# Dealing out a gated block matmul by matmul in an attention kernel, with a new order of the work on GpSimd

## The chip, the cores and the metric

The kernel runs on one core of a Trainium2 chip. The metric is the device time in microseconds (us) of one execution, as the median of several runs. A run is called slow when it is over 1.5% above the fastest run of the same kernel. Engines are called PE (TensorE; PEld is its weight load), DVE (VectorE), ACT (ScalarE), POOL (GpSimd) and SP (SyncE, which issues DMAs). The granted clock is the share of its full clock that PE was given.

## The reference

Eight batches of attention with twelve heads (448 rows, 64 columns), q and k normalized by their root mean square; the heads, put side by side, feed a gated two-layer block whose gate mixes the rows.

```python
q_n, k_n = rmsnorm(q, g_q), rmsnorm(k, g_k)
attn = softmax(q_n @ k_n.T / 8)                 # per head
x = heads_side_by_side(attn @ v)                # (8, 448, 768)
h = relu(x @ w_in)                              # w_in 768 x 1024
u, v = h[..., :512], h[..., 512:]
v_n = (v - mean(v)) / sqrt(var(v) + 1e-6)       # over the 512 columns
v_s = w_spatial @ v_n + b_spatial[:, None]      # mixes the 448 rows
out = (u * v_s) @ w_out                         # w_out 512 x 768
```

## The kernel before

Heads are handled in 24 groups `G` of four, and each group in four steps `n`; one step is a round of the loop over `t`, with `G, n = divmod(t, 4)`. Twelve steps are a batch. Step `t` does the scores and the exponential of one head; around it, the loop queues, in program order on every engine, the preparation of later groups, the sums and values of the group before, and the gated block of the batch before.

A group's q and k go through five stages: `squares` (POOL), `reduce` (DVE), `rstd` (ACT), `scaled` (POOL), then a transpose by DMA; k has a last scaling by column, `k_scale` (DVE). The pieces that the argument touches:

```python
def load_v(b):                                   # 672 KB, issued by POOL
    pool.dma_start(out=t..., in_=v[b]...)

def squares(G, i, ..., eng=None):                # i = 0: q, 1: k
    (eng or pool).tensor_tensor(out=t, in0=x, in1=x, op=ALU.mult)
def reduce(G, i, ...):
    dve.tensor_reduce(out=sqs[G, l0][:, i, :], in_=sqt.pop((G, i, l0))..., op=ALU.add)
def scaled(G, i, ..., eng=None):
    (eng or pool).tensor_tensor(out=t..., in0=raw[G, i, l0]..., in1=rst[G, l0]..., op=ALU.mult)
def transpose_dma(G, i):
    sync.dma_start_transpose(out=t..., in_=nrm[G, i, 0]...)
def k_scale(G):                                  # bf16, from and to SBUF
    dve.tensor_scalar(out=kT, in0=krs.pop(G), scalar1=g2_col, ..., op0=ALU.mult)

def ln_apply(b):                                 # vn: bf16, from and to SBUF, four times
    for c in range(NC):
        dve.tensor_scalar(out=vn_t[b % 2][0:P, c, :], in0=vs[b][:, c, :],
                          scalar1=sts[b][:, c, 0:1], scalar2=rvs[b][:, c:c + 1],
                          op0=ALU.subtract, op1=ALU.mult)
```

The order inside the loop, steady stage:

```python
if n == 3 and G > 2 and G % NG == 0 and G // NG + 1 < B:      # NG = 3 groups a batch
    load_v(G // NG + 1)
A, R, T, K = G + 3, G + 2, G + 2, G + 1
if n == 2 and 5 <= K < NGT:  k_scale(K)
if n == 2 and 6 <= A < NGT:  squares(A, 0)
if n == 3 and 6 <= A < NGT:  squares(A, 1); reduce(A, 0)
if n == 0 and 6 <= R < NGT:  reduce(R, 1)
if n == 1 and 6 <= T < NGT:  rstd(T); scaled(T, 0); scaled(T, 1); transpose_dma(T, 0); transpose_dma(T, 1)
# then: sums at n == 0, values at n == 1 and 2, and the gated block in twelve unequal parts, one a step
```

The softmax here doesn't subtract the row's maximum and nothing guards it: scores larger than these inputs give would overflow.

## Time and profile before

| | before |
|---|---|
| time, median of 4 runs | 337.65 us (336.75 to 339.86) |
| span of the profiled run (fast), mean granted clock | 335.8 us, 0.937 |
| one batch in the steady stage, from exponential to exponential | 35.16 us |
| PE busy in such a batch | 33.64 us |

The prediction below shows the lines and how to read them. One more view, the group of `vn` in the list of groups (busy us, mean ns of one, idle before):

```profile
L331 DVE TENSOR_SCALAR vn<-vs,mv,rv 112x512 bf16<-112x512 bf16 x32 | 13.6, 483 | 0.7 <-ACT rv L326 0.6
```

### The profile page before, as it was taken

The numbers are of one execution on the slowest core, as the hardware profiler recorded it, in microseconds if no ns is written. First come the engines' busy times: TensorE is split into PE (matmuls) and PEld (weight loads), VectorE is DVE, ScalarE is ACT, GpSimd is POOL, SyncE is SP. The second block draws the span as 40 slices with busy tenths as digits, with TensorE's granted clock in tenths as the row PEclk, the third lists the DMA queues.
The fourth block names the chain that finished last, engine by engine and source line by source line (L and its number), as shares of the span: only waits on it lengthen the run. The fifth ranks groups of instructions, "written<-read, shape, count | busy, mean of one in ns | idle before, by whom it ended". The sixth has DMA issues, their size and how long they took to land.

```text
span 335.8 us, 6167 instructions
## 1 busy us (share of the span) xinstructions
PE 298.2 (89%) x2484; PEld 144.9 (43%) x2484; DVE 222.2 (66%) x364; ACT 223.5 (67%) x275; POOL 187.5 (56%) x114
## 2 busy tenths in 40 slices
PE   6757674789999989998999899989998999999993
PEld 6432231434444435443454344434543354435552
DVE  3667754566964977497757877588658964735551
ACT  4648495047877687778687768777877877784331
POOL 5824699747468648665956774795487454000000
PEclk9678595659999999999999999999999999999999
DMA  7993969928458994799389966895679254002205
GB/s 187 241 238 73 187 148 208 207 37 154 111 133 206 190 212 86 206 203 238 68 209 191 183 155 193 174 208 145 171 191 197 49 129 119 27 2 82 84 0 167
DMA packets 75061, 50.45 MB, mean 150 GB/s; under 512 B 36911, under 2 KB 71440, under 8 KB 75032
## 3 DMA queue, kind: packets, MB, share of 16 engines
q1 hardware_dynamic: 61792, 41.76, 53.9%
q0 software_dynamic: 13232, 8.30, 17.9%
q8 instruction: 19, 0.31, 0.4%
q14 instruction: 10, 0.08, 0.1%
q10 hardware_dynamic: 8, 0.00, 0.0%
HBM read 38.58 MB, written 11.01 MB: 148 GB/s over the span
## 4 chain that ended last, share of the span: by engine, by line
POOL 33%; issue 28%; PE 22%; DVE 6%; DMA 6%; ACT 3%; ACTq 0%; POOLq 0%; DVEq 0%; SPq 0%
POOL sqt L167 19%; POOL n L189 11%; PE ps L311 4%; DMA bst<-in_moe_b_spatial_dram 4%; PE ps L364 3%; PE ps L340 3%; PE ps L285 2%; PE pss L234 2%; PE ps L266 2%; ACT et L244 2%; PE ps L350 2%; POOL vt L80 2%; DVE n L189 1%; PE pse L234 1%; PE ps L200 1%
## 5 line engine op out<-in xcount | busy, mean ns | idle before, releaser
L244 ACT ACTIVATE et<-pss 112x1792 bf16<-112x1792 f32 x84 | 139.6, 1662 | 58.4 <-PE pss L234 57.5
L189 POOL TENSOR_TENSOR n<-qf,rs 112x1024 bf16<-112x1024 f32 x22 | 45.9, 2086 | 88.2 <-ACT rs L181 76.4
L173 DVE TENSOR_REDUCE ms<-sqt 112x16 f32<-112x1024 f32 x46 | 55.6, 1215 | 45.2 <-POOL sqt L167 45.2
L364 PE MATMUL ps<-w_out,gt 128*112 128x384 bf16 x256 | 47.6, 330 | 2.9 <-DVE osb L369 2.6
L234 PE MATMUL pss<-qT,kT 64*112 64x448 bf16 x304 | 44.5, 369 | 5.8 <-ACT et L244 5.2
L311 PE MATMUL ps<-w_in_v,xt 128*112 128x512 bf16 x192 | 49.3, 404 | 0.0
L285 PE MATMUL ps<-et,vt 112*32 112x448 bf16 x768 | 46.1, 361 | 0.0
L167 POOL TENSOR_TENSOR sqt<-qf 112x1024 f32<-112x1024 f32 x22 | 42.6, 1934 | 0.0
L167 POOL TENSOR_TENSOR sqt<-kf 112x1024 f32<-112x1024 f32 x22 | 41.7, 1895 | 1.3 <-DMA kf<-in_k_dram 1.2
L340 PE MATMUL ps<-xt,w_in_u 128*128 128x448 bf16 x192 | 40.1, 354 | 0.0
L364 PEld LDWEIGHTS <-gt 128*112 128x112 bf16 x256 | 31.2, 129 | 19.9 <-issue 12.5
L293 DVE TENSOR_TENSOR xt<-ps,rc 128x448 bf16<-128x448 f32 x48 | 29.3, 615 | 15.5 <-PE ps L285 15.5
L189 POOL TENSOR_TENSOR n<-kf,rs 112x1024 bf16<-112x1024 f32 x19 | 38.8, 2040 | 0.0
L311 PEld LDWEIGHTS <-xt 128*112 128x112 bf16 x192 | 24.6, 137 | 21.1 <-issue 9.5
L369 DVE COPY osb<-ps 112x384 f32<-112x384 f32 x46 | 24.4, 552 | 7.6 <-PE ps L364 5.1
L234 PEld LDWEIGHTS <-kT 64*112 64x112 bf16 x304 | 14.9, 124 | 31.7 <-issue 31.4
L285 PEld LDWEIGHTS <-vt 112*32 112x32 bf16 x768 | 16.3, 97 | 25.4 <-issue 17.1
L350 PE MATMUL ps<-w_spT,vn 112*128 112x448 bf16 (+1 forms) x128 | 26.9, 353 | 0.0
L244 ACT ACTIVATE et<-pse 112x896 bf16<-112x896 f32 x24 | 20.5, 913 | 9.6 <-PE pse L234 9.5
L340 PEld LDWEIGHTS <-w_in_u 128*128 128x128 bf16 x192 | 17.1, 98 | 20.9 <-issue 7.2
L266 PE MATMUL ps<-et,ones 112*32 112x448 bf16 x384 | 24.8, 382 | 0.0
L317 DVE BATCH_NORM_STATS2 s<-vs 112x6 f32<-112x512 bf16 x32 | 21.7, 680 | 2.5 <-ACT vs L301 2.5
(59 smaller groups left out, 276.0 us busy)
## 6 DMA issues: line engine op xcount, KB each, us to landing
out_dram<-osb SPq DMA_DIRECT2D x31, 336.0 KB, 3.0
qf<-in_q_dram SPq DMA_DIRECT2D x23, 448.0 KB, 8.1
kf<-in_k_dram SPq DMA_DIRECT2D x23, 448.0 KB, 7.3
vt<-in_v_dram POOLq DMA_DIRECT2D x8, 672.0 KB, 13.1
w_in_v<-in_moe_w_in_dram POOLq DMA_DIRECT2D x4, 192.0 KB, 5.8
w_in_u<-in_moe_w_in_dram POOLq DMA_DIRECT2D x4, 192.0 KB, 8.0
w_out<-in_moe_w_out_dram POOLq DMA_DIRECT2D x1, 768.0 KB, 13.4
f<-in_q_dram SPq DMA_DIRECT2D x2, 224.0 KB, 4.0
```

Source lines behind the costliest of these rows:

```text
L167: (eng or pool).tensor_tensor(out=t, in0=x, in1=x, op=ALU.mult)
L173: dve.tensor_reduce(out=sqs[G, l0][:, i, :], in_=sqt.pop((G, i, l0)).rearrange("p l (c d) -> p (l c) d", d=D), axis=AX.X, op=ALU.add)
L189: (eng or pool).tensor_tensor(out=t.rearrange("p c l d -> p l c d"), in0=raw[G, i, l0].rearrange("p l (c d) -> p l c d", d=D), in1=rst[G, ...
L234: pe.matmul(out=ps[:, h, 0:S], lhsT=kT[64 * h:64 * h + 64, 2 * (n % 2) + c, :], rhs=qT[64 * h:64 * h + 64, :, :], start=True, stop=True)
L244: act.activation(out=exps[G, n // 2][:, c0:c0 + m, :], in_=ps[:, 0:m, 0:S], func=AF.Exp, bias=0.0, scale=1.0)
L266: pe.matmul(out=ps[32 * l:32 * l + 32, 0:S], lhsT=ones, rhs=exps[G, l // 2][:, 2 * c + l % 2, :], start=(c == 0), stop=(c == NC - 1), tile ...
L285: pe.matmul(out=ps[32 * l:32 * l + 32, 0:S], lhsT=vb[b][:, 3 * l + g, c, 32 * half:32 * half + 32], rhs=exps[G, l // 2][:, 2 * c + l % 2, ...
L293: dve.tensor_tensor(out=xts[b][:, 2 * g + half, :], in0=pst.pop((G, half))[:, 0:S], in1=rec[G], op=ALU.mult)
L311: pe.matmul(out=ps[0:P, :], lhsT=xts[b][:, j, c * P:(c + 1) * P], rhs=w_in_v[:, j, :], start=(j == 0), stop=(j == 5))
L340: pe.matmul(out=ps[:, 0:S], lhsT=w_in_u[:, j, 128 * f:128 * f + 128], rhs=xts[b][:, j, :], start=(j == 0), stop=(j == 5))
L350: pe.matmul(out=ps[:, 0:S], lhsT=vn_t[b % 2][0:kp, c, 128 * f:128 * f + 128], rhs=w_spT[0:kp, c, :, :].rearrange("p c s -> p (c s)"), star ...
L364: pe.matmul(out=ps[0:P, 0:384], lhsT=gts[b][:, f, c * P:(c + 1) * P], rhs=w_out[:, f, r], start=(f == 0), stop=(f == 3))
```

## The change

It is meant to make all steps about equally long for PE, so that the exponential of each step hides behind filler work. The gated block becomes a queue of single matmuls, of which each step with `n > 0` takes 2.07 us worth; sums and values become one block at `n == 0`. ACT takes nine of the twenty evacuations of a batch. On POOL, squares of group `G + 3` now come at `n` 0 and 1, ahead of the scalings of group `G + 2` at `n` 2 and 3. Group 4 is transposed by DMA and no longer by PE, and the bias row is needed later. The core of the diff:

```diff
+    def fill(us_of_pe):
+        debt[0] = min(debt[0] + us_of_pe, us_of_pe)
+        while work and (debt[0] > 0 or work[0][0] == 0):
+            cost, fn = work.popleft()
+            debt[0] -= cost
+            fn()
 ...  (gated(b) queues units of v, statistics, u, root, vn, spatial, output; cut)
-        if n == 2 and 6 <= A < NGT:
-            squares(A, 0)
-        if n == 3 and 6 <= A < NGT:
-            squares(A, 1)
-            reduce(A, 0)
-        if n == 0 and 6 <= R < NGT:
-            reduce(R, 1)
-        if n == 1 and 6 <= T < NGT or t == 16:
-            ...rstd(T), both scaled(T), both transpose_dma(T)
+        if G >= 4:
+            if n < 2 and G + 3 < NGT:
+                squares(G + 3, n)
+            if n == 0 and G + 2 < NGT:
+                reduce(G + 2, 0)
+                reduce(G + 2, 1)
+            if n == 1 and G + 2 < NGT:
+                rstd(G + 2)
+            if n >= 2 and G + 2 < NGT:
+                scaled(G + 2, n - 2)
+                transpose_dma(G + 2, n - 2)
+            if n == 2 and G + 1 < NGT:
+                k_scale(G + 1)
 ...
-        if moe:                      # twelve unequal parts
-            if s == 0:
-                unit_v(b, 0, dve)
-                unit_v(b, 1, dve)
-            ...
+        if t >= 12:
+            if n == 2 and G % NG == 0 and t < NST:
+                gated(G // NG - 1)
+            if n > 0 and t < NST:
+                fill(2.07)
```

More of the change, by code (lines that the diff above doesn't have):

```diff
@@ L1 @@
 import math
+from collections import deque
 from contextlib import ExitStack
@@ L294, in xt_store, with pick @@
                           op=ALU.mult)
-    us, vs, sts, gts, osb = {}, {}, {}, {}, {}
+    us, vs, sts, rvs, gts, osb = {}, {}, {}, {}, {}, {}
+    quota = [0]
+    def pick():
+        if quota[0] > 0:
+            quota[0] -= 1
+            return act
+        return dve
     def relu(eng, out, in_):
@@ L303, in relu, with unit, one, unit_v @@
             dve.tensor_relu(out=out, in_=in_)
-    def unit_v(b, c, eng):
-        if c == 0:
-            vs[b] = m_pool.tile([P, NC, DH], BF, name="vs")
-            sts[b] = m_pool.tile([P, NC, 2], FP, name="mv")
-        ps = ps_w.tile([128, 512], FP, name="ps")
-        for j in range(6):
+    def unit(cost, mms, done):
+        cell = {}
+        def one(i):
+            if i == 0:
+                cell[0] = ps_w.tile([128, 512], FP, name="ps")
+            mms(cell[0], i)
+            if i == n - 1:
+                done(cell[0])
+        n, each = cost
+        return [(each, lambda i=i: one(i)) for i in range(n)]
+    def unit_v(b, c):
+        def mms(ps, j):
+            if c == 0 and j == 0:
+                vs[b] = m_pool.tile([P, NC, DH], BF, name="vs")
+                sts[b] = m_pool.tile([P, NC, 2], FP, name="mv")
             pe.matmul(out=ps[0:P, :], lhsT=xts[b][:, j, c * P:(c + 1) * P],
                       rhs=w_in_v[:, j, :], start=(j == 0), stop=(j == 5))
-        relu(eng, vs[b][:, c, :], ps[0:P, :])
+        return unit((6, 0.222), mms, lambda ps: relu(pick(), vs[b][:, c, :], ps[0:P, :]))
     def stats(b, c):
@@ L318, in stats @@
         dve.bn_aggr(out=sts[b][:, c, :], in_=s6)
-    rvs = {}
     def ln_rstd(b):
@@ L333, in ln_apply, with unit_u, mms @@
                               op0=ALU.subtract, op1=ALU.mult)
-    def unit_u(b, f, eng):
-        if f == 0:
-            us[b] = m_pool.tile([128, 4, S], BF, name="us")
-        ps = ps_w.tile([128, 512], FP, name="ps")
-        for j in range(6):
+    def unit_u(b, f):
+        def mms(ps, j):
+            if f == 0 and j == 0:
+                us[b] = m_pool.tile([128, 4, S], BF, name="us")
             pe.matmul(out=ps[:, 0:S], lhsT=w_in_u[:, j, 128 * f:128 * f + 128],
                       rhs=xts[b][:, j, :], start=(j == 0), stop=(j == 5))
-        relu(eng, us[b][:, f, :], ps[:, 0:S])
+        return unit((6, 0.196), mms, lambda ps: relu(pick(), us[b][:, f, :], ps[:, 0:S]))
     def unit_s(b, f):
-        if f == 0:
-            gts[b] = m_pool.tile([128, 4, S], BF, name="gt")
-        ps = ps_w.tile([128, 512], FP, name="ps")
-        for c in range(NC):
+        def mms(ps, c):
+            if f == 0 and c == 0:
+                gts[b] = [m_pool.tile([128, S], BF, name=f"gt{i}") for i in range(4)]
             kp = 113 if c == NC - 1 else P
@@ L352, in unit_s, with done, unit_o @@
                       start=(c == 0), stop=(c == NC - 1))
-        dve.tensor_tensor(out=gts[b][:, f, :], in0=ps[:, 0:S], in1=us[b][:, f, :], op=ALU.mult)
+        def done(ps):
+            dve.tensor_tensor(out=gts[b][f], in0=ps[:, 0:S], in1=us[b][:, f, :], op=ALU.mult)
+        return unit((4, 0.196), mms, done)
     out_c = [out[b].rearrange("(p c) m -> c p m", c=NC) for b in range(B)]
-    def unit_o(b, i, eng, split=False):
+    def unit_o(b, i, split=False):
         c, half = divmod(i, 2)
-        if half == 0:
-            osb[b, c] = o_pool.tile([P, DM], FP, name="osb")
@@ L361, in unit_o, with mms @@
         r = slice(384 * half, 384 * half + 384)
-        ps = ps_w.tile([128, 512], FP, name="ps")
-        for f in range(4):
-            pe.matmul(out=ps[0:P, 0:384], lhsT=gts[b][:, f, c * P:(c + 1) * P],
-                      rhs=w_out[:, f, r], start=(f == 0), stop=(f == 3))
-        if eng is act:
-            act.activation(out=osb[b, c][:, r], in_=ps[0:P, 0:384], func=AF.Copy, bias=0.0, scale=1.0)
-        else:
-            dve.tensor_copy(out=osb[b, c][:, r], in_=ps[0:P, 0:384])
-        if split:
-            sync.dma_start(out=out_c[b][c][:, r], in_=osb[b, c][:, r])
-        elif half == 1:
-            sync.dma_start(out=out_c[b][c], in_=osb[b, c])
+        def mms(ps, f):
+            if half == 0 and f == 0:
+                osb[b, c] = o_pool.tile([P, DM], FP, name="osb")
+            pe.matmul(out=ps[0:P, 0:384], lhsT=gts[b][f][:, c * P:(c + 1) * P],
+                      rhs=w_out[:, f, r], start=(f == 0), stop=(f == 3))
@@ new lines, in done, with bias_row @@
+        def done(ps):
+            if pick() is act:
+                act.activation(out=osb[b, c][:, r], in_=ps[0:P, 0:384], func=AF.Copy, bias=0.0, scale=1.0)
+            else:
+                dve.tensor_copy(out=osb[b, c][:, r], in_=ps[0:P, 0:384])
+            if split:
+                sync.dma_start(out=out_c[b][c][:, r], in_=osb[b, c][:, r])
+            elif half == 1:
+                sync.dma_start(out=out_c[b][c], in_=osb[b, c])
+        return unit((4, 0.169), mms, done)
+    def bias_row():
+        dve.tensor_copy(out=w_spT[96:113, NC - 1, :, :],
+                        in_=bst[96:113, :].rearrange("q (p c) -> q c p", c=NC))
@@ new lines, with gated @@
+    work = deque()
+    def gated(b):
+        work.extend(unit_v(b, 0) + unit_v(b, 1) + [(0, lambda: stats(b, 0))])
+        work.extend(unit_v(b, 2) + [(0, lambda: stats(b, 1))])
+        work.extend(unit_v(b, 3) + [(0, lambda: stats(b, 2)), (0, lambda: stats(b, 3))])
+        work.extend(unit_u(b, 0) + unit_u(b, 1) + [(0, lambda: ln_rstd(b))])
+        work.extend(unit_u(b, 2) + [(0, lambda: ln_apply(b))])
+        work.extend(unit_u(b, 3))
+        if b == 0:
+            work.append((0, bias_row))
+            work.extend((0.5, lambda sc=sc: w_sp_unit(sc)) for sc in range(NC))
+        for f in range(4):
+            work.extend(unit_s(b, f))
+        o0, o1 = unit_o(b, 0), unit_o(b, 1)
+        work.extend(o0[:3] + o1[:3] + o0[3:] + o1[3:])
+        for i in range(2, 8):
+            work.extend(unit_o(b, i, b == B - 1 and i >= 6))
@@ L376 @@
+    def fill(us_of_pe):
[4 more added lines that the diff above has]
+            fn()
+    debt = [0.0]
     NGT = B * NG
@@ L404 @@
         G, n = divmod(t, 4)
-        b, s = divmod(t - 15, 12)
-        moe = b >= 0 and b < B - 1
+        quota[0] = (0, 1, 1, 1)[n] if t < NST else 2
         if t < 12:
@@ L437 @@
             reduce(2, 1)
+            squares(3, 0)
+            squares(3, 1)
         elif t == 5:
             rstd(2)
-            scaled(2, 0)
+            scaled(2, 0, eng=dve)
             scaled(2, 1, eng=dve)
-            squares(3, 0)
-            squares(3, 1, eng=dve)
             load_w_in(1)
+        elif t == 8:
+            squares(4, 0)
+            squares(4, 1)
+            load_w_in(0)
+            load_v(1)
         elif t == 9:
-            scaled(3, 0)
+            rstd(3)
+            scaled(3, 0, eng=dve)
             scaled(3, 1, eng=dve)
-            load_w_in(0)
-            squares(4, 0)
-            load_v(1)
-            squares(4, 1)
+        elif t == 11:
             load_w_sp()
@@ L455 @@
             reduce(4, 1)
+            squares(5, 0)
+            squares(5, 1)
             load_w_out()
@@ L458 @@
             rstd(4)
-            scaled(4, 0)
+            scaled(4, 0, eng=dve)
+            transpose_dma(4, 0)
             scaled(4, 1, eng=dve)
+            transpose_dma(4, 1)
         elif t == 14:
-            squares(5, 0)
-            squares(5, 1)
+            squares(6, 0)
         elif t == 15:
+            k_scale(4)
             reduce(5, 0)
             reduce(5, 1)
-        A, R, T, K = G + 3, G + 2, G + 2, G + 1
-        if n == 2 and 5 <= K < NGT:
-            k_scale(K)
-        if n == 2 and 6 <= A < NGT:
-            squares(A, 0)
-        if n == 3 and 6 <= A < NGT:
-            squares(A, 1)
-            reduce(A, 0)
-        if n == 0 and 6 <= R < NGT:
-            reduce(R, 1)
-        if n == 1 and 6 <= T < NGT or t == 16:
-            T = 5 if t == 16 else T
-            rstd(T)
-            scaled(T, 0)
-            scaled(T, 1)
-            transpose_dma(T, 0)
-            transpose_dma(T, 1)
-        if moe:
-            if s == 1:
-                stats(b, 0)
-            elif s == 2:
-                stats(b, 1)
-            elif s == 3:
-                stats(b, 2)
-                stats(b, 3)
-                ln_rstd(b)
-            elif s == 4:
-                ln_apply(b)
-        if 0 < G <= NGT:
+        elif t == 16:
+            rstd(5)
+            scaled(5, 0)
+            transpose_dma(5, 0)
+            scaled(5, 1)
+            transpose_dma(5, 1)
+            squares(6, 1)
+        if G >= 4:
[11 more added lines that the diff above has]
+                k_scale(G + 1)
+        if 0 < G < NG:
             if n == 0:
@@ L505 @@
                 xt_store(G - 1, n - 1)
-        if t == 15:
-            dve.tensor_copy(out=w_spT[96:113, NC - 1, :, :],
-                            in_=bst[96:113, :].rearrange("q (p c) -> q c p", c=NC))
-        if t < 4:
-            dummies(8)
-        if 15 <= t < 19:
-            w_sp_unit(t - 15)
-        if moe:
-            if s == 0:
-                unit_v(b, 0, dve)
-                unit_v(b, 1, dve)
-            elif s == 1:
-                unit_v(b, 2, dve)
-            elif s == 2:
-                unit_v(b, 3, dve)
-            elif s == 3:
-                unit_u(b, 0, act)
-            elif s == 4:
-                unit_u(b, 1, act)
-                unit_u(b, 2, act)
-            elif s == 5:
-                unit_u(b, 3, dve)
-            elif s == 6:
-                unit_s(b, 0)
-                unit_s(b, 1)
-            elif s == 7:
-                unit_s(b, 2)
-                unit_s(b, 3)
-            elif s == 8:
-                unit_o(b, 0, dve)
-                unit_o(b, 1, act)
-                unit_o(b, 2, dve)
-            elif s == 9:
-                unit_o(b, 3, dve)
-                unit_o(b, 4, dve)
-            elif s == 10:
-                unit_o(b, 5, dve)
-                unit_o(b, 6, act)
-            else:
-                unit_o(b, 7, dve)
-        if t == 15:
-            transposes(4, 0)
-            transposes(4, 1)
+        elif NG <= G and n == 0:
+            sums(G - 1)
+            recip(G - 1)
+            if t < NST:
+                values(G - 1, 0)
+                values(G - 1, 1)
+                xt_store(G - 1, 0)
+                xt_store(G - 1, 1)
+        if t >= 12:
[3 more added lines that the diff above has]
+                fill(2.07)
+        if t >= NST:
+            if t == NST:
+                fill(1.0)
+                values(NGT - 1, 0)
+                xt_store(NGT - 1, 0)
+                fill(1.0)
+                values(NGT - 1, 1)
+                xt_store(NGT - 1, 1)
+                fill(1.0)
         if t < 12:
@@ L559 @@
                 transposes(G + 1, 1)
+            elif t < 4:
+                dummies(8)
             if t + 1 < 12:
@@ L564 @@
                 reduce(3, 1)
-            if t == 8:
-                rstd(3)
-    b = B - 1
-    for c in range(NC):
-        unit_v(b, c, act)
-        stats(b, c)
-    ln_rstd(b)
-    for f in range(4):
-        unit_u(b, f, act)
-    ln_apply(b)
-    for f in range(4):
-        unit_s(b, f)
-    for i in range(8):
-        unit_o(b, i, (act, dve)[i % 2], split=(i >= 6))
+    gated(B - 1)
+    while work:
+        quota[0] = 1
+        for _ in range(9):
+            if work:
+                work.popleft()[1]()
 _INS = ['q', 'k', 'v', 'g_q', 'g_k', 'moe_w_in', 'moe_w_spatial', 'moe_b_spatial', 'moe_w_out']
```

## The prediction

> **What bounds the kernel now.** The kernel walks 96 steps: four of each of the 24 groups of four heads, twelve of each batch. A step is four score matmuls into one four-bank tile `pss`, one exponential of it on ACT, and filler work for TensorE. I read the page's busy table first, then windows, the chain that ended last, the waits and the timelines.
>
> ```profile
> PE 298.2 (89%) x2484; PEld 144.9 (43%) x2484; DVE 222.2 (66%) x364; ACT 223.5 (67%) x275; POOL 187.5 (56%) x114
> ```
>
> ```profile
> 47.00:57.60 10.60, 5.96 (x61) 2.19 (x60) 4.73 (x5) 7.99 (x8) 10.43 (x8) 0.70 1.27 218
> 57.60:69.60 12.00, 7.39 (x40) 4.10 (x44) 7.66 (x12) 0.03 (x1) 7.13 (x5) 0.64 1.04 183
> ...
> 122.80:157.96 35.16, 33.64 (x292) 15.65 (x288) 25.71 (x43) 26.64 (x33) 24.00 (x13) 1.00 0.87 188
> ...
> 280.00:305.00 25.00, 25.00 (x206) 11.15 (x203) 13.92 (x28) 18.43 (x18) 1.44 (x1) 1.00 0.19 47
> ```
>
> The columns after the length are busy us of PE, weight load, DVE, ACT and POOL, then granted clock, DMA share and GB/s. Three stages show. From about 87 us one batch takes 35.16 us, of which TensorE is busy 33.64 at full clock: it is the bound, and no other engine exceeds 27. Before 57.6 the exponentials and the preparation of q and k set the pace, with TensorE at a low clock. Between them lies a hole of 12 us in which ACT does nothing:
>
> ```profile
> 52.67 12.84 DMA bst<-in_moe_b_spatial_dram
> 65.53 0.56 DVE w_spT L507
> ```
>
> ```profile
> ACT et L244 <- PE pss L234: 57.5, 49, 12.0
> ```
>
> In order of time the chain shows a small bias row landing 12.84 us after its issue; DVE, in order, waits for it at step 15, and the copies of q and k for step 16 stand behind it. The wait list counts that as one wait of 12.0 us.
>
> In the busy stage I take the cost of work from the same chain, where it runs on TensorE without a break (start, length, work):
>
> ```profile
> 280.37 2.73 PE ps L311 x12
> 283.10 0.52 PE pss L234 x4
> 283.61 0.87 PE ps L266 x16
> 284.48 1.43 PE ps L311 x6
> ...
> 303.42 2.09 PE ps L364 x12
> ...
> 306.38 1.44 PE ps L364 x8
> ...
> 311.79 5.18 PE ps L311 x24
> 316.96 4.54 PE ps L340 x24
> 321.50 3.06 PE ps L350 x16
> ```
>
> Twelve value-half matmuls of the gated part (L311) take 2.73, six take 1.43: 0.216 each and about 0.13 over. L364: 0.1625 each and 0.14 over. So each change of kind of work costs about 0.13 us beside the streaming. The two gaps left in a batch are
>
> ```profile
> 132.58 1.46 PE L364 MATMUL ps<-w_out,gt 128*112 128x384 bf16 x8 [0.39 <-DVE osb L369]
> ...
> 154.64 0.59 PE L234 MATMUL pss<-qT,kT 64*112 64x448 bf16 x4 [1.03 <-ACT et L244]
> ```
>
> The second is a step whose exponential started late, as ACT, in order, sat in the gated part's variance logarithm.
>
> **What the Trainium skill says.** "TensorE: Matmul & The Clock Gate", section Back-to-back issue gap, gives N / 2.4 GHz + 2.5 ns warm: 216, 189 and 162.5 ns for 512, 448 and 384 columns; the chain agrees (5.18/24 = 216, 4.54/24 = 189). "TensorEngine Tiling (Array Packing)", section Key Properties, says that changing the tiling mode drains the engine. Scores use 64-row tiles, sums and values 32-column tiles, the gated part the whole array; the 0.13 us fits, though no row isolates it. "TensorE: Matmul & The Clock Gate", section What's actually happening, has two clocks, 1.2 GHz after an idle window and 2.4 GHz when busy: the twelve L311 matmuls at 60.5 us took 4.92, against 2.73 later. "GPSIMD Engine Reference", section Specifications, says that POOL shares SBUF access with DVE when DVE has two SBUF inputs: a scaling on POOL takes 2.94 us beside one on DVE, 1.90 alone.
>
> **The change, part by part.**
>
> *Steady stage.* No matmul is added or removed. In a batch the gated part streams 5.18 + 4.54 + 3.06 + 32 x 0.1625 = 17.98 us. Before, it stood in twelve unequal blocks, sums and values in nine blocks of 0.87, and scores in twelve of 0.51: 17.98 + 7.83 + 6.12 + 12 x 0.13 = 33.5, plus gaps of about 1.5, makes 35.0 (measured 35.16, so the sum can be trusted). After: sums and values are one block of 48 at step 0 of a group, (0.87 - 0.13)/16 x 48 = 2.22 + 0.13; the gated part is nine blocks of about 2.0 + 0.13 at the other steps. The steps are then 2.86 and 2.64 long. The shortest possible step (scores, exponential, back) is 2.34, as 137.42 to 139.76 on ACT shows, so equal shares hide the exponential everywhere. Sum: 17.98 + 6.66 + 6.12 + 1.56 + 0.15 for changes inside a share = 32.5.
>
> ACT gets nine of the twenty evacuations instead of five: about +2.0, so 28.7 of 32.5. At step 1 of a group it has exponential 1.56, rstd 0.7, relu 0.5 = 2.8 against 2.64. The 0.15 by which the next exponential starts late fits the 0.3 of slack. DVE falls to about 24. One new wait I find by following the built program's order: `vn` (four times 0.48) stands on DVE behind both stores of xt, which wait for the reciprocal at 3.3 us into the group; the first spatial matmuls reach `vn` about 0.6 early. So 33.1 a batch, 2.1 less.
>
> *The waits on PSUM.* I feared that a unit left half done across step 0 would block the four rotating `ps` banks. The built program shows that it doesn't: the first unit after the block takes the bank of the sums, freed by an early logarithm; the next ones wait for the two xt stores, which are done in time.
>
> *The head.* The bias row is now needed in the gated part at about step 20, so the 12 us hole goes; q and k of group 4 come by DMA transposes (2.9 us each in the DMA table). Walking the order with durations of the trace: step 8 starts 1.5 us earlier (no squares on DVE in front), step 12 only 0.5 earlier. At step 13 the rstd ends at 51.5, two scalings end at 53.9, the transposes at 57.3, k's scaling at 58.2; cold TensorE finishes two shares by 59. So step 16 begins near 59.5 instead of 69, 9.5 earlier. Then part is lost again: the second squares of group 6 stand on POOL behind the scalings of group 5 and end near 68, while DVE, in order, waits to reduce them ahead of the stores of group 3. I get about 5 us of stalls at steps 17 to 19 and 1 more at 21; but the kernel before is slow there too. Step 22's scores start at 81.4 in my walk against 89.6 before: 8.2 gained.
>
> *From step 22 to the sums of step 96:* 74 steps, 6.17 batches x 33.1 = 204.2, against 215.0 before. That puts those sums at 285.6, against 304.6.
>
> *Tail.* As before: leftover shares, then a whole gated part alone. The four separate `gt` tiles let the output matmuls start with the last product pending, which saves the 0.7 us gap at 324.6. Length 31.2 - 0.7 = 30.5.
>
> Sum: 285.6 + 30.5 = 316.1 of span, and 2.4 more for the time (338.2 against a span of 335.8): 318.5. I say 318.
>
> **The rivals.** (1) *ACT becomes the bound.* It would be busy 28.7 of 32.5, and in order. If evacuations wait at its head for unfinished units, each exponential behind slips past the slack of 0.3. For: step 1 is overfull. Against: each relu's unit ends inside the share, before the next scores. It would give back 0.2 us a step, 15 in all: about 331. (2) *DVE or POOL in order starve the steps.* The stall I see at steps 17 to 19 might repeat in every group: a reduction waiting for POOL, a key scaling waiting for a transpose, with the stores behind. For: the new block needs both xt stores at once, and POOL now starts squares only after the reductions. Against: POOL has 7.8 us of work plus a load issue in a group of 10.9, and the transposes have about 6 us before their use. At 1 us a group it is 20 us: no gain in the steady stage, 330 or more. (3) *The head loses nothing at 17 to 19*, or the two-step clock is up earlier: 5 us better, 313.
>
> **Range and chances.** The head is a hand walk (3 us either way), the steady stage a sum that reproduces the kernel before within 0.2 us a batch, but with waits I may have missed; most misses make it slower. Predicted 318, range 311 to 327. Faster by over 2% means below 331.4: 0.93. Within 2%: 0.06. Slower: 0.01.
>
> **What would show it.** Steps right: a batch of about 33.1 us in steady state with TensorE busy over 97% of it; no 12 us wait of ACT; step 16's exponential near 60 us and step 22's near 82; spatial matmuls (L369) waiting about 0.6 us for `vn` once a batch; ACT near 28.7 us a batch; a tail near 30.5. Wrong: ACT waits with TensorE idle in each group, `ps` matmuls waiting for xt stores or for relus, DVE waiting for POOL squares in each group, or a clock below 1.00 in the steady stage.

## The result, and the profile after

The kernel after takes 363.82 us (360.71 to 367.35, 4 runs) against 337.65 in the same rounds: slower, ratio 1.0734, 95% interval 1.062 to 1.0847. Ratios here are the mean time of one kernel's fast runs over that of the other's of the same rounds, so not quite the ratio of the medians, which are of all four runs (e3 has one slow run among them, e10 two). The profiled run of the kernel after is a slow one (span 365.6 us, clock 0.902; the fast ones have spans of 358.9 to 363.8), and no fast one was profiled.

Busy time by engine on the page after, then three windows: the two of the head that the prediction shows of before, and one steady batch (length, busy us of PE, weight load, DVE, ACT, POOL, granted clock, DMA share, GB/s):

```profile
PE 305.8 (84%) x2460; PEld 149.4 (41%) x2460; DVE 227.2 (62%) x343; ACT 233.4 (64%) x295; POOL 178.9 (49%) x112
```

```profile
47.00:57.60 10.60, 7.91 (x66) 3.50 (x67) 7.28 (x11) 6.51 (x7) 5.71 (x6) 0.73 1.22 213
57.60:69.60 12.00, 6.19 (x35) 2.71 (x37) 2.46 (x4) 3.55 (x4) 0.67 (x1) 0.78 1.06 175
100.17:140.55 40.38, 35.36 (x288) 16.64 (x283) 26.78 (x39) 28.17 (x34) 23.99 (x13) 0.92 0.76 155
```

The last window stops 0.25 us short of the next exponential, so this batch takes 40.6 us, and the next one 40.4. PE idles 40.38 - 35.36 = 5.0 us in the window, against 1.5 before, and is busy 1.7 longer at a lower clock. The hole of 12 us in the head is still a hole: ACT is busy 3.55 of 12. The list of waits after (us in all, times, longest) has three entries that the kernel before has not; the first stays at 67.8 us in e3 below, so it is not the loss in itself:

```profile
POOL sqt L168 <- DVE ms L174: 101.8, 15, 14.1
...
DVE kT L223 <- DMA kr<-n: 24.9, 6, 9.5
...
PE ps L369 <- DVE vn L351: 22.2, 15, 1.5
```

I follow one batch through the timelines (start, length, engine, line, work, and in brackets the idle time before it and what ended it). POOL first:

```profile
105.28 2.38 POOL L190 TENSOR_TENSOR n<-qf,rs 112x1024 bf16<-112x1024 f32 x1 [0.29 <-ACT rs L182]
107.62 0.98 POOL L81 DMA_DIRECT2D vt<-in_v_dram  x1
108.61 1.92 POOL L190 TENSOR_TENSOR n<-kf,rs 112x1024 bf16<-112x1024 f32 x1
...
124.71 1.89 POOL L168 TENSOR_TENSOR sqt<-qf 112x1024 f32<-112x1024 f32 x1 [4.85 <-DVE ms L174]
126.56 1.89 POOL L168 TENSOR_TENSOR sqt<-kf 112x1024 f32<-112x1024 f32 x1
128.41 1.95 POOL L190 TENSOR_TENSOR n<-qf,rs 112x1024 bf16<-112x1024 f32 x1
130.32 1.95 POOL L190 TENSOR_TENSOR n<-kf,rs 112x1024 bf16<-112x1024 f32 x1
```

The load of v stands between the scaling of q and that of k. The chain that ended last shows what becomes of the transpose of k, issued at 111.01 behind that load:

```profile
111.01 9.89 DMA kr<-n
120.90 0.02 issue
120.93 0.46 DVE kT L223
```

DVE, in order, waits for it; the statistics and reductions behind it come late, so POOL starts its squares only at 124.71 and then works without a break to 132.27. DVE reaches `vn` just there:

```profile
120.93 0.46 DVE L223 TENSOR_SCALAR kT<-kr,g_col 128x896 bf16<-128x896 bf16 x1 [3.48 <-DMA kr<-n]
...
123.42 2.33 DVE L174 TENSOR_REDUCE ms<-sqt 112x16 f32<-112x1024 f32 x2
...
127.26 5.48 DVE L351 TENSOR_SCALAR vn<-vs,mv,rv 112x512 bf16<-112x512 bf16 x4
```

Four `vn` take 5.48 us (1.34, 1.99, 1.99 and 0.40) in place of 4 x 0.48. PE gets its operands one by one:

```profile
128.66 0.36 PE L369 MATMUL ps<-w_spT,vn 112*128 112x448 bf16 x1 [1.27 <-DVE vn L351]
130.57 0.56 PE L369 MATMUL ps<-w_spT,vn 112*128 112x448 bf16 x1 [1.55 <-DVE vn L351]
132.48 0.56 PE L369 MATMUL ps<-w_spT,vn 112*128 112x448 bf16 x1 [1.35 <-DVE vn L351]
...
133.89 3.69 PE L369 MATMUL ps<-w_spT,vn 113*128 113x448 bf16 x10
```

The starts 128.66, 130.57 and 132.48 are POOL's ends 128.41, 130.32 and 132.27 plus 0.21 to 0.25. PE idles 4.2 us; the ten matmuls that follow take 0.37 each where the fast clock gives 0.19.

In the head, the transpose of group 4's k was issued at 58.03 and DVE had it at 67.26, so step 16's exponential starts at 68.80, almost as late as before (69.58). SP's timeline, then DVE's:

```profile
58.03 4.61 SPq L212 DMA_TRANSPOSE kr<-n  x1
...
67.26 0.45 DVE L223 TENSOR_SCALAR kT<-kr,g_col 128x896 bf16<-128x896 bf16 x1 [9.54 <-DMA kr<-n]
```

### The profile page after: what moved, and what is told of

The parts are those of the page before. It is cut to its first block, busy times and chain, and to the rows that moved or that the text cites. A ratio compares the mean times of both kernels' runs of the same rounds, so it can differ in the third digit from the quotient of the medians.

```text
span 365.6 us, 6124 instructions
## 1 busy us (share of the span) xinstructions
PE 305.8 (84%) x2460; PEld 149.4 (41%) x2460; DVE 227.2 (62%) x343; ACT 233.4 (64%) x295; POOL 178.9 (49%) x112
## 4 chain that ended last, share of the span: by engine, by line
PE 40%; DMA 16%; DVE 14%; issue 13%; POOL 11%; ACT 4%; SPq 1%; POOLq 0%; DVEq 0%
DMA kr<-n 13%; PE ps L387 12%; PE ps L369 10%; DVE vn L351 7%; PE pss L235 6%; POOL sqt L168 5%; PE ps L286 4%; PE ps L332 3%; DMA kf<-in_k_dram 3%; PE ps L359 3%; PE ps L267 2%; ACT et L245 2%; DVE xt L294 2%; DVE s L339 2%; POOL n L190 2%
## 5 line engine op out<-in xcount | busy, mean ns | idle before, releaser
L369 PE MATMUL ps<-w_spT,vn 112*128 112x448 bf16 (+1 forms) x128 | 42.2, 470 | 22.2 <-DVE vn L351 22.2
L235 PE MATMUL pss<-qT,kT 64*112 64x448 bf16 x320 | 49.9, 392 | 6.5 <-DVE kT L223 6.2
L190 POOL TENSOR_TENSOR n<-qf,rs 112x1024 bf16<-112x1024 f32 x19 | 38.6, 2030 | 26.7 <-issue 14.4
L190 POOL TENSOR_TENSOR n<-kf,rs 112x1024 bf16<-112x1024 f32 x19 | 36.4, 1916 | 0.1
L374 DVE TENSOR_TENSOR gt<-ps,us 128x448 bf16<-128x448 f32 x32 | 20.0, 625 | 25.2 <-PE ps L369 24.8
L369 PEld LDWEIGHTS <-vn 112*128 112x128 bf16 (+1 forms) x128 | 14.3, 121 | 48.6 <-DVE vn L351 27.7
L286 PEld LDWEIGHTS <-vt 112*32 112x32 bf16 x768 | 21.4, 102 | 25.6 <-issue 8.9
L351 DVE TENSOR_SCALAR vn<-vs,mv,rv 112x512 bf16<-112x512 bf16 x32 | 31.5, 1044 | 0.0
L394 DVE COPY osb<-ps 112x384 f32<-112x384 f32 x38 | 21.2, 558 | 16.1 <-PE ps L387 14.5
L223 DVE TENSOR_SCALAR kT<-kr,g_col 128x896 bf16<-128x896 bf16 x20 | 12.9, 646 | 24.9 <-DMA kr<-n 24.9
## 6 DMA issues: line engine op xcount, KB each, us to landing
vt<-in_v_dram POOLq DMA_DIRECT2D x8, 672.0 KB, 12.6
```

The costliest lines, as they stand in the source:

```text
L190: (eng or pool).tensor_tensor(out=t.rearrange("p c l d -> p l c d"), in0=raw[G, i, l0].rearrange("p l (c d) -> p l c d", d=D), in1=rst[G, ...
L235: pe.matmul(out=ps[:, h, 0:S], lhsT=kT[64 * h:64 * h + 64, 2 * (n % 2) + c, :], rhs=qT[64 * h:64 * h + 64, :, :], start=True, stop=True)
L286: pe.matmul(out=ps[32 * l:32 * l + 32, 0:S], lhsT=vb[b][:, 3 * l + g, c, 32 * half:32 * half + 32], rhs=exps[G, l // 2][:, 2 * c + l % 2, ...
L369: pe.matmul(out=ps[:, 0:S], lhsT=vn_t[b % 2][0:kp, c, 128 * f:128 * f + 128], rhs=w_spT[0:kp, c, :, :].rearrange("p c s -> p (c s)"), star ...
```

## The experiments

Two theories. **D**: the load of v delays the transpose of k by some 7 us once a batch, and everything behind it is late. **P**: POOL, while it works without a break, holds up DVE instructions of one kind, `vn` here. A rival to both is that the equal shares themselves starve or stall PE. Each experiment is a small edit of the kernel after, of the kernel before, or of an experiment ahead of it; all gave correct results. "Batches" are the times from exponential to exponential over steps 36 to 48, 48 to 60 and 60 to 72.

### e1_vn_early: vn out of POOL's way

```diff
-        work.extend(unit_u(b, 0) + unit_u(b, 1) + [(0, lambda: ln_rstd(b))])
-        work.extend(unit_u(b, 2) + [(0, lambda: ln_apply(b))])
+        work.extend(unit_u(b, 0) + unit_u(b, 1) + [(0, lambda: ln_rstd(b)), (0, lambda: ln_apply(b))])
+        work.extend(unit_u(b, 2))
```

> The changed kernel with the four vn (normalise) instructions moved on DVE from behind the xt stores to straight behind the variance root, ahead of the reductions, when POOL is idle. Theory P (vn is held up by POOL instructions that use the same SBUF interface): vn falls from 1.04 us each to about 0.5, the waits of the spatial matmuls for vn (22.2 us in the changed kernel) fall below 5, the cold clock behind them goes, and the time falls by 4 to 5 us in each of six batches: about 335 to 342 us. Rival S (the equal shares and the one block of sums and values are themselves to blame, through PSUM banks or the order on ACT): vn is only a symptom, the time stays over 355.

Measured: 328.2 us (326.65 to 329.87), ratio 0.9715; batches 33.29, 34.07, 33.05. The key scaling still waits 22.6 us in all for the transposes, as in the kernel after. So the late transpose by itself costs little in the steady stage (e3, without it, is 0.6 to 1.5 us a batch shorter); `vn` beside POOL costs most. I had put it at 335 to 342.

### e2_v_late: the load of v behind the squares

```diff
-        if n == 3 and G > 2 and G % NG == 0 and G // NG + 1 < B:
-            load_v(G // NG + 1)
 ...
+            if n == 1 and G % NG == 1 and G // NG + 1 < B:
+                load_v(G // NG + 1)
```

> The changed kernel with the load of the next batch's v moved from between the scalings of q and k to behind the squares of the following group. Theory D (the DMA transpose of k lands 9 to 10 us after its issue once a batch because it stands behind or beside that 672 KB load): the transposes of k land in about 3 to 4 us in all groups of the steady stage, the wait of the key scaling for them (24.9 us in six waits) falls to about 12 (the one of 9.5 at step 15 stays, it has other neighbours), and the time falls by 1.5 to 3 us in each of six batches, to about 346 to 355. vn stays at about 1.0 us. Rival S: no change beyond 2 us from 362.

Measured: 327.12 us (324.63 to 327.58), ratio 0.9668; batches 32.65, 33.0, 32.97. The lists of groups and of waits:

```profile
L351 DVE TENSOR_SCALAR vn<-vs,mv,rv 112x512 bf16<-112x512 bf16 x32 | 11.0, 405 | 0.0
```

```profile
DVE kT L223 <- DMA kr<-n: 12.6, 1, 12.6
```

No steady batch waits for a transpose (the one left is in the head), and `vn` is short though nothing was done to it. My expectation, that `vn` would stay near 1.0 and the time at 346 to 355, was wrong: in this kernel the place of the load, and with it the late transpose, is what brings POOL's run and `vn` together.

### e3_both

The diffs of e1 and e2 together.

> Both edits. P and D together: a batch of 33 to 34 us as first predicted, 320 to 328 us in all. S: over 350.

Measured: 323.24 us (321.16 to 327.34), ratio 0.9547; batches 32.42, 32.58, 32.42. This is the steady stage that the change was meant to have, 0.7 better than the 33.1 I had worked out. The profiled run is a slow one, but the fast profiles of e5 and e12 have the same batches to 0.01 us. The median of the three fast runs is 321.75.

### e4_pool_order: equal shares with the old order on POOL

The block at `if G >= 4` gives way to the order of the kernel before; the shares stay.

```diff
-            if n < 2 and G + 3 < NGT:
-                squares(G + 3, n)
-            ...
+        if n == 2 and 6 <= A < NGT:
+            squares(A, 0)
+        if n == 3 and 6 <= A < NGT:
+            squares(A, 1)
+            reduce(A, 0)
+        if n == 0 and 6 <= R < NGT:
+            reduce(R, 1)
+        if n == 1 and 6 <= R < NGT:
+            ...rstd(R), both scaled(R), both transpose_dma(R)
```

> The changed kernel with the part 'squares a group ahead of scalings' undone for the steady stage: squares, reductions, roots, scalings, transposes and key scalings placed at the steps of the kernel before, equal shares and the one block kept. P and D: POOL is idle when vn runs and the transposes of k come ahead of the load of v, so vn is about 0.5 to 0.6 us, the key scaling hardly waits in the steady stage, and the time is 320 to 330. S: stays over 350, as equal shares and the one block are still there.

Measured: 355.48 us (354.05 to 355.89), ratio 1.0514; batches 37.75, 38.17, 38.52. A miss. `vn` and the transposes are in order (0.405 us; median landing 3.0 us), but PE now waits for the gated products `gt`:

```profile
DVE ms L174 <- POOL sqt L168: 41.3, 22, 3.3
...
PE ps L387 <- DVE gt L374: 16.7, 6, 3.0
```

The reduction at step 3 of a group waits on DVE for squares just queued on POOL. That wait is no larger than in the kernel before (45.2 us, 27 times, longest 3.0), but here the products that PE needs stand behind it. By this reading the equal shares need the squares ahead; no run tests it alone, and the key scaling, too, now takes up to 1.7 us beside POOL.

### e5_weights_early and e8_weights_v: the head

The head's transpose was issued beside the load of `w_out` (768 KB at 53.43). Both kernels issue what is left to load earlier. e5 is e3 with this diff; e8 is e2 with it, so the kernel after with nothing but loads moved.

```diff
         elif t == 5:
             ...
             load_w_in(1)
+            load_w_in(0)
+            load_v(1)
+            load_w_sp()
         elif t == 8:
             ...
-            load_w_in(0)
-            load_v(1)
+            load_w_out()
-        elif t == 11:
-            load_w_sp()
         elif t == 12:
             ...
-            load_w_out()
```

> The kernel with both edits (323.2 us), and the loads of the gated part's weights and of the second batch's v issued by POOL at steps 5 and 8, 10 us earlier, so that they are down before the transposes of group 4. Theory D for the head (step 16 starts at 69 to 70 us, not near 60, because the transpose of k lands 9 to 12 us after its issue beside the 768 KB load of w_out): the transposes of group 4 land in 3 to 5 us, step 16's exponential starts at 60 to 63, and the time falls by 6 to 9 us to 314 to 318. Rival H (something else sets step 16: cold TensorE or the copies on DVE): step 16 stays at 67 or later and the time over 321.

> The same without the move of vn (the changed kernel with only the loads of v and of the weights moved, nothing touched on the compute engines' order beyond POOL's issues). If loads beside the transposes are the whole cause, this alone reaches the first prediction: step 16 at 60 to 63 us, batches of about 32.8 us, 316 to 321 us in all. If the order of vn matters in itself it stays 3 us or more above the run with both.

Measured: e5 319.03 us (318.28 to 320.62), ratio 0.9454; e8 321.44 (320.97 to 321.8), ratio 0.951. Step 16 starts at 61.83 and 62.81, against 68.80. So most of the head's hole, too, was a transpose that landed late; which of the loads delayed it was not separated. Moving loads alone takes the kernel after from 363.8 to 321.4.

### e6_pool_probe: POOL work put beside vn

In e3 the last batch's `vn` has no POOL work near. Here six useless squares, started by that batch's statistics, are put on POOL.

```diff
+    def pool_probe():
+        t = first.tile([P, NC, 2], FP, name="pr")
+        pool.tensor_tensor(out=t, in0=sts[B - 1], in1=sts[B - 1], op=ALU.mult)
+        for i in range(6):
+            squares(NGT - 1, i % 2)
 ...  (the last batch's queue is rebuilt with pool_probe behind its statistics; cut)
```

> The kernel with both edits and seven useless instructions on POOL (one tiny, six squares of 1.9 us, their results unused, the output still right) in the tail, where POOL is otherwise idle, running while the last batch's vn, gt and output copies run on DVE. Theory P: each vn (bf16, both operands in SBUF) waits for the POOL instruction in flight: 1.5 to 2.0 us each instead of 0.41, and they end where POOL's squares end; the gt multiplications and output copies, which read PSUM, keep their 0.62 and 0.56. The time rises by 3 to 6 us. Rival: vn stays at 0.41 and the slow ones in the changed kernel had another cause, such as waits on ACT's root counted as busy time.

Measured: one run, 330.5 us (state unknown). Timeline of DVE in e3, then in e6:

```profile
310.48 1.37 DVE L351 TENSOR_SCALAR vn<-vs,mv,rv 112x512 bf16<-112x512 bf16 x4
```

```profile
306.14 0.62 DVE L312 TENSOR_SCALAR us<-ps 128x448 bf16<-128x448 f32 x1 [0.73 <-PE ps L359]
306.68 6.71 DVE L351 TENSOR_SCALAR vn<-vs,mv,rv 112x512 bf16<-112x512 bf16 x4
314.04 0.62 DVE L374 TENSOR_TENSOR gt<-ps,us 128x448 bf16<-128x448 f32 x1 [0.65 <-PE ps L369]
```

The same four instructions on the same data take 1.37 and 6.71; the products `gt`, which read PSUM, stay at 0.62 in the middle of POOL's squares (which ran from 305.65 to 317.00). P is shown directly for `vn`, and `gt` is shown not to be of its kind. What makes the kind is argued below with the Trainium skill; no run varies it.

### e7_before_pool and e10_before_pool_v: the new order in the kernel before

e7 is the kernel before with the new order on POOL: of the change's diff above, the lines from `if n == 2 and 6 <= A` to `scaled` and `transpose_dma` at `n >= 2`, and no more. e10 is e7 with the diff of e2.

> One part of the change alone: the kernel before with only the new order on POOL in the steady stage (squares ahead of scalings, both reductions at the first step of a group, scalings at the third and fourth with their transposes), its unequal shares and separate blocks kept. D and P: the load of v now stands between the two scalings, so the transpose of k lands late once a batch, and vn at the fourth step of a group meets POOL's scalings: 1.5 us or more each, batches of 37 to 41 us and 345 to 370 us in all. Rival S (shares and block are needed for the loss): within 2% of 338.

> The kernel of e7_before_pool (the kernel before with only the new order on GpSimd, 350.47 us) with the value load issued behind the squares, as in e2_v_late. Theory D with P (the late transposes of k line GpSimd's work up beside vn): the transposes land in about 3 us again, no wait of over 1 us for them in steady batches, vn below 600 ns, steady batches of 35 to 36 us instead of about 38, and 335 to 342 us, as the kernel before. Rival (the new order on GpSimd costs something of its own in the kernel with uneven shares): vn and transposes recover but batches stay at 37 or more and the time at 345 or above.

Measured: e7 350.47 us (348.95 to 352.36), ratio 1.0376, batches 38.03, 37.93, 39.32. So this part alone makes a slower kernel. That it fell into my range was luck: I had put `vn` at 1.5 us or more, and it took 0.44 on average and was held in the first batch alone; the waits for transposes are 9.4 us in all. ACT waits 19.7 us for the statistics behind the key scaling, against 11.5 in the kernel before; the rest was not followed. e10 362.33 (357.52 to 365.87), ratio 1.0626, batches 40.34, 39.0, 39.98: worse (two of its four runs are slow, the fast ones took 361.47 and 357.52), where D with P said 335 to 342 and the rival 345 or above. The transposes were on time (at most 5.3 us, no steady wait) and `vn` took 0.41. DVE and POOL in e10:

```profile
194.98 0.69 DVE L303 TENSOR_SCALAR vs<-ps 112x512 bf16<-112x512 f32 x1
195.59 4.36 DVE L222 TENSOR_SCALAR kT<-kr,g_col 128x896 bf16<-128x896 bf16 x1
199.87 0.68 DVE L317 BATCH_NORM_STATS2 s<-vs 112x6 f32<-112x512 bf16 x1
```

```profile
194.93 0.98 POOL L80 DMA_DIRECT2D vt<-in_v_dram  x1
195.92 1.91 POOL L189 TENSOR_TENSOR n<-qf,rs 112x1024 bf16<-112x1024 f32 x1
197.79 1.90 POOL L189 TENSOR_TENSOR n<-kf,rs 112x1024 bf16<-112x1024 f32 x1
```

The key scaling, 0.44 us when POOL is still, took 4.36 and ended 0.26 after POOL's last. Two statistics stand behind it, and ACT, in order, waits for them 8.2 us at the longest with an exponential behind:

```profile
ACT lv L325 <- DVE mv L318: 31.8, 8, 8.2
```

So D fell as the cause in general, and the rival's numbers came true. Being on time can be worse than being late, if it puts such an instruction beside POOL's run.

### e11_k_on_act and e12_head_k_act: the key scaling off DVE

e9_reduce_late had come first: e5 with group 6's reductions one step later, to remove a DVE wait of 3.14 us in the head.

```diff
-            if n == 0 and G + 2 < NGT:        # both reductions
+            if n == (1 if G == 4 else 0) and G + 2 < NGT:
-            if n == 1 and G + 2 < NGT:        # root; group 7's squares go to n = 1, 2 likewise
+            if n == (2 if G == 4 else 1) and G + 2 < NGT:
```

> The kernel of e5_weights_early (319.03 us) with one thing moved in the first batch: the two reductions of group 6 stand one step later (step 17, behind the second store of group 3's transposed features), so that the in-order VectorE is not held in step 16 or 17 for GpSimd's squares. If the rest of the head's loss is that wait (3.14 us at 69.85 in e5's trace): steps 16 to 22 take about 22 to 23.5 us instead of 25.5, and the kernel 314 to 317 us. If the loss there is the key scaling of group 5 beside GpSimd (4.83 us) or the engines' plain work: within 1 us of e5.

Measured: 319.25 us (319.05 to 319.34), no change. The wait shrank only to 2.15 us, now behind the stores of group 3, and the key scaling of group 5 then started beside POOL and took 5.88 us at 73.72, against 4.83 in e5. That, with e10, led to the last two:

```diff
+        if G % NG == 2:            # e11, on e10;   e12, on e5:  if G == 5
+            act.activation(out=kT, in_=krs.pop(G), func=AF.Identity, bias=0.0, scale=g2_col)
+        else:
             dve.tensor_scalar(out=kT, in0=krs.pop(G), scalar1=g2_col, scalar2=None, op0=ALU.mult)
```

> The kernel of e10_before_pool_v (362.33 us) with one key scaling in three (groups 2, 5, 8 and so on), the one that stood beside GpSimd's unbroken run and took 4.36 us on VectorE at 195.59, done by ScalarE instead; loads, order and the other two as they were. Theory P (a VectorE instruction of the two-port kind is held while GpSimd works, whichever it is, vn or kT): the statistics behind it are on time, ScalarE's wait for them (31.8 us in all) nearly vanishes, the batches fall from 39 to 40.3 us to 35 to 37, and the kernel takes 332 to 343 us, though ScalarE does about 1 us more per batch. Rival (the new order costs something else when the shares are uneven): batches stay above 38 and the time above 350.

> The kernel of e5_weights_early (319.03 us) with the key scaling of group 5 alone, which took 4.83 us on VectorE at 73.66 beside three GpSimd instructions, done by ScalarE (about 1 us there). Theory P: steps 16 to 22 take 21 to 23.5 us instead of 25.5 and the kernel 315 to 317.5 us. Rival (as in e9_reduce_late, where removing one wait of the head only brought up the next): within 1 us of 319.

Measured: e11 329.14 us (327.82 to 330.39), ratio 0.9718, batches 33.81 three times: better than expected, some 30 us less than e10's fast runs for one scaling in three moved. ACT's wait for the statistics fell from 31.8 us in all to 1.0. P, with the key scaling as the second victim, stands. e12 317.09 (315.75 to 317.54), ratio 0.9358, the fastest of all, but its expectation failed in part. Steps 16 to 22 took 84.64 - 60.25 = 24.4 us, not 21 to 23.5; e5 needed 25.5. Step 12 had already started 1.8 us earlier than in e5, where the two programs are the same, so of the 2 us at most about one is the edit's. The same steps take 24.3 to 25.5 in e1, e3, e5 and e8, which keep the scaling on DVE, so e12 shows no gain there beyond that spread. `vn` of batch 0 fell into the place of the key scaling (e12, DVE):

```profile
73.96 3.82 DVE L354 TENSOR_SCALAR vn<-vs,mv,rv 112x512 bf16<-112x512 bf16 x4 [0.83 <-ACT rv L349]
```

### What the parts are worth

| order on POOL | gated part | `vn` or `kT` held by POOL for long | kernel | batch, us |
|---|---|---|---|---|
| old | unequal | no (`kT` 1.43 once) | before | 35.16 |
| old | equal | no (`kT` up to 1.7; products wait behind reductions) | e4 | 37.8 to 38.5 |
| new | unequal | `kT` 4.36 | e10 | 39.0 to 40.3 |
| new | unequal | no (`vn` 1.30, `kT` 1.44 once each) | e11 | 33.81 |
| new | equal | `vn` 5.48 for four | after (slow run) | 40.4 to 41.4 |
| new | equal | no (`kT` up to 1.43) | e3 | 32.4 to 32.6 |

Once nothing is held up for long, the new order is worth 35.16 - 33.81 = 1.35 us a batch (e11 also has one key scaling on ACT), and the equal shares, with the one block and ACT's nine evacuations, 33.81 - 32.42 = 1.4 more.

## Why the prediction was wrong, point by point

- **Shares, block and ACT: right.** The prediction feared ACT, at 28.7 of 32.5 us, as a bound; it is busy 28.17 in a batch of the kernel after, and e3's 32.4 shows that it hides. Sums and values in one block cost nothing unforeseen. The batch was predicted at 33.1 and e2 has 32.65 to 33.0.
- **The step that failed in the steady stage** is the one new wait: "`vn` (four times 0.48) stands on DVE [...] the first spatial matmuls reach `vn` about 0.6 early". The place was right, the duration was not: 5.48 us for the four (mean of all 1.044), with PE idle for 4.2 and slow after. I had cited the page "GPSIMD Engine Reference", section Specifications, for the access that POOL and DVE share, and applied it to a scaling on DVE only; the row there names the kind of DVE instruction that uses two ports as well. "VectorE: DVE Perf Modes" (The perf-mode tier table) gives a bf16 `tensor_scalar` on SBUF the 4x mode, which the SBUF page counts as two-port; no run here shows the mode itself. The Trainium skill page "SBUF — State Buffer", section Who interferes with whom, goes further: the shared pair is taken for a whole instruction and the other engine is fully blocked. e6 agrees (1.37 to 6.71 us), and so do the ends of `vn` at POOL's ends.
- **Why it did not show in the kernel before**, from whose `vn` group I took the 0.48: there it falls at the end of POOL's run (the batch at 120.04 took 1.80 for four, the first of them 0.83 and the others 0.40, and POOL's last square ended at 120.73). So the 0.48 was a mean that already held a part of the wait. A duration measured in one order was used in another order.
- **The second failed step** is "the transposes have about 6 us before their use", with which I set rival 2 aside. Once a batch a transpose took 9 to 10 us to land, as its own order put the load of v (12.6 us median landing) just ahead of it. The diff did not touch that load, and I did not look at what stood between the two scalings. The Trainium skill page "DMA: Bandwidth & Descriptors", section Queues, rings and completion order, says that a DMA engine takes turns between the queues it has work for, packet by packet; the numbers here fit that, and no run isolates it.
- **The head failed by the same term**: "the transposes at 57.3" took 2.9 us of landing from a quiet stretch; beside the load of `w_out` it was about 9. The walk was early too: it had the two scalings done at 53.9, the trace at 57.7. With the weights earlier, step 16 starts at 61.8, near the 59.5 of the walk. The later stall at steps 17 to 19 was foreseen: e5 shows 3.14 us of DVE waiting for POOL, and the kernel after 4.13.
- **The rivals.** Rival 2, that DVE or POOL in order starve the steps, is what happened, once a batch and not once a group. It was given 330 or more, and the chances left 0.07 for all of not faster. Of the two arguments against it the first held in size (POOL is busy 23.99 us a batch, 8.0 a group) but did not ask what stands beside that work; the second was a landing time taken from other neighbours.
- **Sizes.** Steps 24 to 95 took 334.18 - 100.17 = 234.0 us in the profiled run, against 71/12 x 33.1 = 195.8 predicted: 38 us. Step 22's scores came some 11 us later than in the walk. Together that is nearly all of the 49.5 us between the predicted span of 316.1 and 365.6, of which 2 to 7 us belong to this slow run and not to the kernel. The tail was right: from the sums of step 96 to the end it took 29.4 us against 30.4 before, 1.0 less where 0.7 was predicted. Two small readings were off: PE's gap at 324.6 is 0.30 us of idle time, and from span to time it is 1.8 us in one run (337.58 against 335.8), not 2.4.

What stays open: why such an instruction at times gets in after one POOL instruction (`vn` in the kernel after, most key scalings) and at times is kept out over two or three in a row. It is not the instruction: in e12 a `vn` was kept out over the end of one scaling and the whole next one. Nor is it POOL's issue of the load of v alone, near which the long ones of e5, e9 and e10 stand: the key scalings at 81.22 in the kernel after (3.83 us) and at 76.23 in e4 (4.67) have no such issue near. Also open is what is left of the head, about 24 us for steps 16 to 22 where the walk had about 22; e12 shows only that the hold moves on to the next instruction.

## What to carry to other kernels

Before taking a VectorE duration into a new order, ask whether the instruction is of the kind that was held here (the bf16 scalings from SBUF to SBUF, `vn` and `kT`) and what GpSimd does at its new place; if GpSimd works there without a break, count GpSimd's instructions, not VectorE's. If work is spread over more steps, look at what the program already had in the gaps, above all large DMA issues, and list the transfers that then run beside a small one with a deadline. And when a good change measures slow, try the cheapest reorderings first: here moving loads alone, without undoing any part, turned 7% slower into 5% faster.

## What the Trainium skill lacked or had wrong

- "SBUF — State Buffer", Who interferes with whom: whoever issues first takes the shared pair for its instruction. It does not say who gets it next. Here three of four `vn` waited for one POOL instruction of 1.9 us each (5.48 us for the four), but elsewhere a key scaling or a `vn` was kept out over two or three consecutive ones (4.36 us in e10, 5.88 in e9, alone 0.44).
- "DMA: Bandwidth & Descriptors": no landing time for a small SBUF-to-SBUF transpose beside a large load. Here it is 2.9 us at the least and up to 10.1 behind a load of 672 KB.
- "TensorE: Matmul & The Clock Gate", Back-to-back issue gap: it gives 131 ns per matmul of 512 columns as the sustained pace of a real stream, and 216 as that of an isolated one. This trace streams at 216 (24 in 5.18 us).
- "TensorEngine Tiling (Array Packing)", Key Properties: it names the drain at a change of tiling but no size; about 0.13 us per change of work fits the rows of the kernel before, as an estimate.
